# Pair writes of a routed MoE kernel moved to slots of their own, with GpSimd in text order

## Chip, core and metric

One core of a Trainium2 chip runs the whole kernel. The metric is the device time of one execution in microseconds (us), as the median over the runs shown. Engines: PE (TensorE; PEld is its weight load), DVE (VectorE), ACT (ScalarE), POOL (GpSimd) and SP (SyncE, which issues the ordinary DMAs).

## What is computed

A decayed linear attention over 4 x 768 tokens feeds a two-layer MLP, and its output x (3072 tokens x 384) goes through a mixture of eight experts, each token to its best one:

```python
kt, vt, rt, wt = (k[:, :, t], v[:, :, t], r[:, :, t], w[:, :, t])
cur = np.einsum('bhd,bhe->bhde', u[None] * kt, vt)
y[:, :, t] = np.einsum('bhd,bhde->bhe', rt, state + cur)
state = wt[:, :, :, None] * state + np.einsum('bhd,bhe->bhde', kt, vt)
...
h = x @ w_in
g = np.maximum(h, 0.0) + alpha * np.minimum(h, 0.0)
x = g @ w_out
...
expert_idx = np.argmax(x @ w_gate, axis=1)
gate_w = probs[np.arange(N), expert_idx]
out[mask] = gate_w[mask, None] * (np.maximum(x[mask] @ w1[e], 0.0) @ w2[e])
```

## The kernel before, in words

**Tiles and stages.** The tokens form 24 attention tiles of 128, numbered 0 to 23, and 8 blocks of three tiles, numbered 0 to 7. A prologue computes tiles 0 to 2. The main loop then has 128 MLP steps, 16 for each block; a step is one piece of 128 hidden units: nine matmuls of the first layer (`p1`, L584, into `ph`), the activation (ACT `gn` L587, DVE `gt` L589, ACT `gh` L595, DVE `gl` L597), and two steps later nine matmuls of the second layer (`p2`, L610, into `py`). Every product is made of high and low parts, so weights and activations each come as a pair (`wih`/`wil`, `woh`/`wol`, `gh`/`gl`). After the MLP the experts run in units of 256 or 128 tokens.

**Slots.** A step has two slots, and other work is hung on slot numbers with `at_slot`: the attention of the tiles of the next block, the conversion of the MLP weights during block 0, and the routing of the block just finished. For tile t the attention steps that matter here are: `r` on GpSimd (L292, written as dm<-dm,ex); the scores on PE (L348), ACT copies `at` (L356) that GpSimd masks (L360); `rk` on GpSimd (L312 and L313), which DVE reduces to `c` (L318), which GpSimd multiplies into `cv` (L328); the state `st`, added on DVE (L394) and multiplied by the decay `pm` on GpSimd (L395); `pm` itself on ACT (L339), in a single buffer, so that the next `pm` waits for `st`; the output `x` on DVE (L424), which PE transposes into `px` (L435).

**Routing of a block.** `gate_block` (L462) hangs four things on slots: the gate logits (on DVE as `sink` L489 for blocks 0 to 5, on PE for the last two), `route`, `rank` and `scatter`. `scatter` computes for each of the block's 384 tokens its row in the DRAM table `metad` (`slot`, L543) and the pair of token number and gate weight (`meta`, L547 to L549), and then GpSimd writes the pairs with three indirect DMAs (L551), one for each tile. I call these sends 0, 1 and 2. They write the same DRAM tensor, so each waits until the one before it has landed. `slot` and `meta` come from a pool with two buffers per name.

**Order.** Inside `manual_schedule(engines=...)` the engines named keep the order of the program text; a scheduler orders the rest ahead of the run. In the main loop `ORDER1` names PE alone until six steps before the end of the MLP; from there `ORDER2` names PE and DVE. On the chip each engine takes its instructions in the order so fixed.

**Weights in block 0.** The MLP weights arrive in 16 pieces j (even: first layer, odd: second layer). Each goes through ACT (`v`, L203), three DVE operations (L207, L208, L211), ACT (the high part, L224) and DVE or, for odd j, GpSimd (the low part, L229: `wil` or `wol`). Piece j = 8 is first needed by step 8, and so on.

Of the kernel before, what the change touches and what calls it, by code (L numbers as in the profile page):

```python
# [12 lines left out]
I32 = mybir.dt.int32  # L13
# [26 lines left out]
NBLK = NTILE // NB  # L40
# [3 lines left out]
EARLY = -(-((NBLK - 1) * BN - E * (UNIT - 1)) // UNIT)  # L44
LAG = 2
EPE, EDVE = mybir.EngineType.PE, mybir.EngineType.DVE


ORDER0 = None
ORDER1 = {EPE}  # L50
ORDER2 = {EPE, EDVE}
SWITCH = -6

# [1 line left out]

PE_GATES = 2
GV = 4
WARM0 = 16
WL_OFF = 6
LOW_V = range(0, 16, 2)  # L60
# [36 lines left out]
def attention_mlp_moe(ctx, tc, dmaj, tmaj, ub, alpha, w_in, w_out, w_gate, w_gate_b, wexp, out):  # L97
    nc = tc.nc
    vec, act, pool, pe, sp = nc.vector, nc.scalar, nc.gpsimd, nc.tensor, nc.sync
# [5 lines left out]
    mp = ctx.enter_context(tc.tile_pool(name="mp", bufs=2))  # L105
# [7 lines left out]
    ap = att_stack.enter_context(tc.tile_pool(name="ap", bufs=2))  # L113

    x2d = dp.tile([NT + 1, DM], F32, name="x2d")
    metad = dp.tile([NSLOT, 2], I32, name="metad")
# [29 lines left out]
    def warm(n):  # L146

        w = ps_h.tile([128, NP * 96], F32, tag="ph", name="warm")
        for _ in range(n):
            pe.matmul(w, lhsT=ones[:PR, :], rhs=bmask.rearrange("p a e -> p (a e)"), start=True, stop=True)  # L150
# [12 lines left out]
    def w_tiles(g):  # L163
        for lst, nm in ((wi_h, "wih"), (wi_l, "wil")):
            lst.append(wp.tile([128, KC, 1024], F32R, tag="W", name=f"{nm}{g}"))
        for lst, nm in ((wo_h, "woh"), (wo_l, "wol")):
            lst.append(wp.tile([128, 8, DM], F32R, tag="W", name=f"{nm}{g}"))
# [294 lines left out]
    def gate_block(blk, x2, g0):  # L462
        nt = NB
        t0 = blk * NB
        cx = {}

        def tr(j):
            pa = ps_a.tile([128, KC, 128], F32, tag="pa", name="px2")
            for c in range(KC):
                pe.transpose(pa[:, c, :], x2[:, j, 128 * c : 128 * c + 128], ident)  # L470
            xt = mp.tile([128, KC, 128], F32, tag="x2t", name="x2t")
            act.copy(xt, pa)
            cx[j] = xt

        def lg(j):
            pl = ps_a.tile([128, E], F32, tag="pa", name="plg")
            for c in range(KC):
                pe.matmul(pl, lhsT=cx[j][:, c, :], rhs=wg_s[:, c, :], start=c == 0, stop=c == KC - 1)
            if j == 0:
                cx["l"] = mp.tile([128, nt, E], F32, tag="lg", name="lg")  # L480
            vec.tensor_copy(cx["l"][:, j, :], pl)

        def lv(j, h):

            if j == h == 0:
                cx["l"] = mp.tile([128, nt, E], F32, tag="lg", name="lg")
            sink = mp.tile([128, DM], F32, tag="x2t", name="sink")
            for e in range(E // 2):
                vec.scalar_tensor_tensor(  # L489
                    out=sink,  # L490
                    in0=x2[:, j, :],
                    scalar=1.0,
                    in1=wgb_t[h][:, e, :],
                    op0=ALU.mult,
                    op1=ALU.mult,
                    accum_out=cx["l"][:, j, h * (E // 2) + e : h * (E // 2) + e + 1],
                )

        def small(name, dt=F32, w=E):
            return mp.tile([128, nt, w], dt, tag="g_" + name, name="g_" + name)  # L500

        def bc(t):
            return t.to_broadcast([128, nt, E])

        iob = iom.rearrange("p (o e) -> p o e", o=1).to_broadcast([128, nt, E])

        def route():
            l = cx["l"]
            m = small("m", w=1)
            vec.tensor_reduce(out=m, in_=l, axis=AX.X, op=ALU.max)  # L510
            sh, eq = small("sh"), small("eq")
            vec.tensor_tensor(out=eq, in0=l, in1=bc(m), op=ALU.is_equal)
            vec.tensor_tensor(out=eq, in0=eq, in1=iob, op=ALU.mult)
            mi = small("mi", w=1)
            vec.tensor_reduce(out=mi, in_=eq, axis=AX.X, op=ALU.min)
            oh = small("oh", BF16)
            vec.tensor_tensor(out=oh, in0=bc(mi), in1=iob, op=ALU.is_equal)
            ac = mp.tile([128, nt + 1, E], BF16, tag="g_ac", name="g_ac")
            pool.tensor_copy(ac[:, 0, :], acc_t[-1])
            for j in range(nt):  # L520
                pool.tensor_tensor(out=ac[:, j + 1, :], in0=ac[:, j, :], in1=oh[:, j, :], op=ALU.add)
            acc_t.append(ac[:, nt, :])
            vec.tensor_tensor(out=sh, in0=l, in1=bc(m), op=ALU.subtract)
            act.activation(sh, sh, AF.Exp)
            cx.update(sh=sh, mi=mi, oh=oh, ac=ac)

        def rank():
            oh, ac = cx["oh"], cx["ac"]
            pr = ps_a.tile([128, nt, E], F32, tag="pa", name="prk")
            fl = "p a e -> p (a e)"  # L530
            pe.matmul(pr.rearrange(fl), lhsT=tri, rhs=oh.rearrange(fl), start=True, stop=False)
            pe.matmul(pr.rearrange(fl), lhsT=ones, rhs=ac[:, 0:nt, :].rearrange(fl), start=False, stop=True)
            cx["pr"] = pr

        def scatter():
            sh, mi, oh, pr = cx["sh"], cx["mi"], cx["oh"], cx["pr"]
            rk = small("rk")
            vec.tensor_tensor(out=rk, in0=pr, in1=oh, op=ALU.mult)
            pos = small("pos", w=1)
            vec.tensor_reduce(out=pos, in_=rk, axis=AX.X, op=ALU.add)  # L540
            vec.tensor_scalar(mi, mi, float(NT), float(E * NT), op0=ALU.mult, op1=ALU.add)
            slot = small("slot", I32, 1)
            vec.tensor_tensor(out=slot, in0=pos, in1=mi, op=ALU.add)  # L543
            se = small("se", w=1)
            vec.tensor_reduce(out=se, in_=sh, axis=AX.X, op=ALU.add)
            vec.tensor_scalar(se, se, 1e-9, None, op0=ALU.add)
            meta = small("meta", I32, 2)  # L547
            pool.tensor_copy(meta[:, :, 0], tokid[:, t0 : t0 + nt])
            vec.reciprocal(out=meta.bitcast(F32)[:, :, 1:2], in_=se)  # L549
            for j in range(nt):  # L550
                pool.indirect_dma_start(  # L551
                    out=metad,
                    out_offset=bass.IndirectOffsetOnAxis(ap=slot[:, j, :], axis=0),
                    in_=meta[:, j, :],
                    in_offset=None,
                )

        g1 = g0 + 7
        if blk < NBLK - PE_GATES:
            for j in range(nt):  # L560
                for h in range(2):
                    at_slot(g0 + 1 + GV * (2 * j + h), lambda j=j, h=h: lv(j, h))
            g1 = g0 + 2 + 6 * GV
        else:
            for j in range(nt):
                at_slot(g0 + 2 + j, lambda j=j: tr(j))
                at_slot(g0 + 4 + j, lambda j=j: lg(j))
        at_slot(g1, route)
        at_slot(g1 + 2, rank)
        at_slot(g1 + 3, scatter)  # L570
        return g1 + 3

    g_t = {}
# [338 lines left out]
    def at_slot(s, fn):  # L912
        todo.setdefault(s, []).append(fn)
# [21 lines left out]
    at_slot(PT0, lambda: w_tiles(0))  # L935
    at_slot(PT0, lambda: warm(WARM0))
    for t, n in PRO_WARM:
# [48 lines left out]
    for i in range(len(steps) + LAG):  # L986
        if i == 0:
            order.close()
            tc.no_sync_barrier()
            order.enter_context(tc.manual_schedule(engines=ORDER1))  # L990
        if i == NM + SWITCH:
# [26 lines left out]
    with tc.For_i(0, nrem, 1) as iv:  # L1018
        tb = qp.tile([1, 1, 2], I32, tag="tb", name="tb", bufs=1)
        sp.dma_start(  # L1020
            out=tb, in_=tabd[:, ds(iv * 2, 2)].rearrange("p (o c) -> p o c", o=1)
# [71 lines left out]
```

## Time and profile before

| | |
|---|---|
| median of 3 runs | 877.07 us (875.84 to 878.21) |
| profiled execution, its own time | 875.71 us |
| span of that execution | 874.0 us |
| mean granted TensorE clock | 0.961 of full speed |
| busy: PE, DVE, ACT, POOL | 820.5, 645.4, 384.3, 293.4 us |

The span runs from the first to the last instruction; the time of the execution is 1.7 us longer. Times in the rows below are counted from the start of the span. The prologue lies at 0 to about 41 us, block 0 of the MLP at 41 to 140, the blocks after it up to about 607, the experts behind. In a timeline row the first number is the start, the second the duration, and the bracket at the end, where there is one, tells how long the engine sat idle before the row and what ended that wait.

### The profile page before, as it was taken

How to read it: one execution, taken by the hardware profiler on the slowest of the kernel's cores; microseconds unless marked ns; L12 is line 12 of the kernel's file. 1: busy time of each engine (PE TensorE's matmuls, PEld its weight loads, DVE VectorE, ACT ScalarE, POOL GpSimd, SP SyncE). 2: the span in 40 equal slices, each digit the busy share in tenths (PEclk: the TensorE clock that was granted, in tenths of full speed). 3: DMA queues.
4: the chain of work that ended last, by engine and by line, in shares of the span. 5: the costliest groups of instructions: out<-in, count | busy, mean ns of one | idle time of the engine just before them, and what ended most of it. 6: DMA issues, size and time to landing. Idle time of an engine off the chain costs nothing. (4 is left out here: it accounts for less than half of the span.)

```text
span 874.0 us, 14602 instructions
## 1 busy us (share of the span) xinstructions
PE 820.5 (94%) x5453; PEld 796.1 (91%) x5453; DVE 645.4 (74%) x1219; ACT 384.3 (44%) x751; POOL 293.4 (34%) x309
## 2 busy tenths in 40 slices
PE   6878789999799999999999999999999999999994
PEld 4768779999799999999999999999899999999993
DVE  6999898977686996896996983446767576776761
ACT  3545343344133433333333432337355556565641
POOL 5474444233332433343423330122224122232301
PEclk8779888999899999999999999999999999999997
DMA  9625534022212321311312300036456668585830
GB/s 281 203 83 171 193 120 148 29 60 86 59 59 60 87 60 60 86 60 60 86 60 59 87 1 1 28 137 242 147 202 240 224 216 293 204 294 204 275 119 21
DMA packets 30513, 111.59 MB, mean 128 GB/s; under 512 B 8229, under 2 KB 11592, under 8 KB 30440
## 3 DMA queue, kind: packets, MB, share of 16 engines
q1 hardware_dynamic: 26088, 100.38, 35.8%
q0 software_dynamic: 4352, 10.26, 3.2%
q8 instruction: 44, 0.72, 0.3%
q14 instruction: 29, 0.24, 0.1%
HBM read 100.95 MB, written 10.45 MB: 127 GB/s over the span
## 5 line engine op out<-in xcount | busy, mean ns | idle before, releaser
L584 PE MATMUL ph<-xth,wih 128*128 128x384 f32 x384 | 138.1, 360 | 8.4 <-DVE gt L589 5.2
L610 PE MATMUL py<-woh,gh 128*128 128x384 f32 x384 | 138.1, 360 | 1.0 <-ACT gh L595 1.0
L584 PE MATMUL ph<-xth,wil 128*128 128x384 f32 x384 | 132.9, 346 | 6.2 <-DVE wil L229 6.2
L595 ACT CAST gh<-gt 128x384 fp32r<-128x384 f32 x128 | 65.6, 513 | 158.5 <-DVE gt L589 158.5
L610 PE MATMUL py<-woh,gl 128*128 128x384 f32 x384 | 131.4, 342 | 1.4 <-DVE gl L597 1.4
L584 PE MATMUL ph<-xtl,wih 128*128 128x384 f32 x384 | 132.3, 345 | 0.0
L610 PE MATMUL py<-wol,gh 128*128 128x384 f32 x384 | 131.2, 342 | 0.0
L597 DVE TENSOR_TENSOR gl<-gt,gh 128x384 fp32r<-128x384 f32 x128 | 91.9, 718 | 33.3 <-ACT gh L595 31.8
L589 DVE SCALAR_TENSOR_TENSOR gt<-gn,oma_s,ph 128x384 f32<-128x384 f32 x128 | 76.4, 597 | 50.3 <-ACT gn L587 50.1
L587 ACT ACTIVATE gn<-ph 128x384 f32<-128x384 f32 x128 | 62.7, 490 | 113.2 <-PE ph L584 110.1
L815 DVE SCALAR_TENSOR_TENSOR gl<-ph,gh 128x256 fp32r<-128x256 f32 x96 | 40.4, 422 | 73.9 <-ACT gh L813 67.2
L489 DVE SCALAR_TENSOR_TENSOR sink<-x,wgb 128x384 f32<-128x384 f32 x144 | 88.1, 634 | 2.1 <-ACT x L621 1.4
L584 PEld LDWEIGHTS ph<-xth,wih 128*128 128x128 f32 x384 | 74.6, 194 | 10.3 <-DVE gt L589 5.8
L810 PE MATMUL ph<-xh,w1h 128*128 128x256 f32 x288 | 81.5, 283 | 1.2 <-DVE gl L815 1.1
L584 PEld LDWEIGHTS ph<-xth,wil 128*128 128x128 f32 x384 | 74.7, 194 | 7.4 <-DVE wil L229 7.4
L884 POOL DMA_INDIRECT out<-ys,meta x28 | 28.5, 1018 | 156.3 <-ACT ys L881 97.5
L810 PE MATMUL ph<-xl,w1h 128*128 128x256 f32 x288 | 80.8, 281 | 0.0
L810 PE MATMUL ph<-xh,w1l 128*128 128x256 f32 x288 | 80.4, 279 | 0.0
L610 PEld LDWEIGHTS py<-woh,gh 128*128 128x128 f32 x384 | 74.7, 195 | 3.0 <-ACT gh L595 1.3
L610 PEld LDWEIGHTS py<-woh,gl 128*128 128x128 f32 x384 | 74.1, 193 | 2.5 <-DVE gl L597 2.5
L584 PEld LDWEIGHTS ph<-xtl,wih 128*128 128x128 f32 x384 | 74.9, 195 | 0.8 <-DVE xtl L446 0.3
L610 PEld LDWEIGHTS py<-wol,gh 128*128 128x128 f32 x384 | 74.6, 194 | 0.0
(211 smaller groups left out, 1906.4 us busy)
## 6 DMA issues: line engine op xcount, KB each, us to landing
raw<-w SPq DMA_DIRECT2D x64, 768.0 KB
dm<-dmaj SPq DMA_DIRECT2D x21, 673.8 KB
tm<-tmaj SPq DMA_DIRECT2D x21, 576.0 KB
raw<-w_out SPq DMA_DIRECT2D x8, 768.0 KB
raw<-w_in SPq DMA_DIRECT2D x7, 768.0 KB
x2d<-x SPq DMA_DIRECT2D x8, 576.0 KB
both<-tmaj SPq DMA_DIRECT2D x3, 576.0 KB
wgb<-w_gate_b SPq DMA_DIRECT2D x2, 768.0 KB
```

The costliest lines, as they stand in the source:

```text
L489: vec.scalar_tensor_tensor(out=sink, in0=x2[:, j, :], scalar=1.0, in1=wgb_t[h][:, e, :], op0=ALU.mult, op1=ALU.mult, accum_out=cx["l"][:, ...
L584: pe.matmul(ph, lhsT=w, rhs=x[:, c, :], start=k == 0, stop=k == 3 * KC - 1)
L587: act.activation(gn, ph, AF.Relu, scale=-1.0)
L589: vec.scalar_tensor_tensor(out=gt, in0=gn, scalar=oma_s[:, f : f + 1], in1=ph, op0=ALU.mult, op1=ALU.add)
L595: act.copy(gh, gt)
L597: vec.tensor_tensor(out=gl, in0=gt, in1=gh.bitcast(F32), op=ALU.subtract)
L610: pe.matmul(y_t[blk][j], lhsT=g[:, sl], rhs=w, start=f == 0 and m == 0, stop=f == NF1 - 1 and m == 2,)
L810: pe.matmul(ph, lhsT=w, rhs=x, start=k == 0, stop=k == 3 * KC - 1)
L815: vec.scalar_tensor_tensor(out=gl, in0=ph, scalar=0.0, in1=gh.bitcast(F32), op0=ALU.max, op1=ALU.subtract)
L884: pool.indirect_dma_start(out=out, out_offset=bass.IndirectOffsetOnAxis(ap=d["meta"][:, j, 0:1], axis=0), in_=ys, in_offset=None, bounds_c ...
```

## The change

Four edits: `slot` and `meta` get one buffer per block (`NBLK` = 8) instead of two; the sends leave `scatter` and become a function of their own; for blocks 0 to 5 send j stands `SEND * j` = 0, 4 and 8 slots behind `scatter`, for the last two blocks all three stay at its slot; and GpSimd joins PE in `ORDER1`, so it keeps the text order up to the switch.

```diff
-ORDER1 = {EPE}
+ORDER1 = {EPE, EPOOL}
...
+SEND = 4
...
-            slot = small("slot", I32, 1)
+            slot = mp.tile([128, nt, 1], I32, tag="g_slot", name="g_slot", bufs=NBLK)
...
-            meta = small("meta", I32, 2)
+            meta = mp.tile([128, nt, 2], I32, tag="g_meta", name="g_meta", bufs=NBLK)
             pool.tensor_copy(meta[:, :, 0], tokid[:, t0 : t0 + nt])
             vec.reciprocal(out=meta.bitcast(F32)[:, :, 1:2], in_=se)
-            for j in range(nt):
-                pool.indirect_dma_start(
-                    out=metad,
-                    out_offset=bass.IndirectOffsetOnAxis(ap=slot[:, j, :], axis=0),
-                    in_=meta[:, j, :],
-                    in_offset=None,
-                )
+            cx.update(slot=slot, meta=meta)
+
+        def send(j):
+            pool.indirect_dma_start(
+                out=metad,
+                out_offset=bass.IndirectOffsetOnAxis(ap=cx["slot"][:, j, :], axis=0),
+                in_=cx["meta"][:, j, :],
+                in_offset=None,
+            )
...
         at_slot(g1 + 3, scatter)
+        for j in range(nt):
+            at_slot(g1 + 3 + (SEND * j if blk < NBLK - PE_GATES else 0), lambda j=j: send(j))
```

The order of PE's instructions stays as it was. Those of GpSimd, and with them those of DVE and ACT, which the scheduler places around it, move. Three places show it; line numbers of the changed kernel are larger by 3 to 5.

**GpSimd at the sends of block 0, before.** `cv` and `r` of tiles 9 and 10 stand ahead of the first row, and the last copy `g_meta` belongs to a later block.

```order
L312 TENSOR_TENSOR rk<-tm 128x384
L313 TENSOR_TENSOR rk<-rk,ub_s 128x384
L551 DMA metad<-g_meta,g_slot 24832x2 x2
L360 AFFINE_SELECT at_2024<-at_2024 128x512
L360 AFFINE_SELECT at_2027<-at_2027 128x512
L551 DMA metad<-g_meta,g_slot 24832x2
L548 COPY g_meta<-tokid 128x3
L395 TENSOR_TENSOR st<-st,pm 112x384
L328 TENSOR_TENSOR cv<-tm,c 128x384
```

**The same place now.**

```order
L551 COPY g_meta<-tokid 128x3
L556 DMA metad<-g_meta,g_slot 24832x2
L331 TENSOR_TENSOR cv<-tm,c 128x384
L363 AFFINE_SELECT at_2022<-at_2022 128x512
L363 AFFINE_SELECT at_2025<-at_2025 128x512
L295 TENSOR_TENSOR dm<-dm,ex 112x512
L556 DMA metad<-g_meta,g_slot 24832x2
L398 TENSOR_TENSOR st<-st,pm 112x384
L315 TENSOR_TENSOR rk<-tm 128x384
L316 TENSOR_TENSOR rk<-rk,ub_s 128x384
L556 DMA metad<-g_meta,g_slot 24832x2
L331 TENSOR_TENSOR cv<-tm,c 128x384
```

The masks of tile 9 and its `st` now stand between the sends and not behind the second and third; the two products `rk` of tile 10 stand behind send 1 and `st`, where they stood ahead of send 0. No copy `g_meta` for a later block stands behind send 2.

**DVE between `st` and `x` of tile 9, before and now.** The sinks are the gate logits of block 0.

```order
L394 TENSOR_TENSOR st<-pv,st 112x384
L489 SCALAR_TENSOR_TENSOR sink,lg<-x_2048,wgb 128x384 x3
L589 SCALAR_TENSOR_TENSOR gt<-gn,oma_s,ph 128x384
L489 SCALAR_TENSOR_TENSOR sink,lg<-x_2048,wgb 128x384 x2
L597 TENSOR_TENSOR gl<-gt,gh 128x384
L489 SCALAR_TENSOR_TENSOR sink,lg<-x_2048,wgb 128x384
L424 TENSOR_TENSOR x<-py,cv 128x384
```

```order
L397 TENSOR_TENSOR st<-pv,st 112x384
L492 SCALAR_TENSOR_TENSOR sink,lg<-x_2046,wgb 128x384 x3
L596 SCALAR_TENSOR_TENSOR gt<-gn,oma_s,ph 128x384
L321 TENSOR_REDUCE c<-rk 128x8
L492 SCALAR_TENSOR_TENSOR sink,lg<-x_2046,wgb 128x384
L604 TENSOR_TENSOR gl<-gt,gh 128x384
L492 SCALAR_TENSOR_TENSOR sink,lg<-x_2046,wgb 128x384
L427 TENSOR_TENSOR x<-py,cv 128x384
```

The reduction `c` of tile 10, which reads `rk` of that tile, now stands ahead of `x` of tile 9. It stood some fifteen rows earlier. The same exchange is found at blocks 2 and 4.

**GpSimd in block 0 of the MLP, before and now** (attention of tiles 3 and 4; `wol` are the low parts of pieces 3, 5 and 7).

```order
L519 COPY g_ac<-acc_117 128x8
L548 COPY g_meta<-tokid 128x3 x2
L328 TENSOR_TENSOR cv<-tm,c 128x384
L312 TENSOR_TENSOR rk<-tm 128x384
L292 TENSOR_TENSOR dm<-dm,ex 112x512
L313 TENSOR_TENSOR rk<-rk,ub_s 128x384
L360 AFFINE_SELECT at_539<-at_539 128x512
L229 TENSOR_TENSOR wol_121<-v_496,woh_120 128x768
L360 AFFINE_SELECT at_542<-at_542 128x512
L395 TENSOR_TENSOR st<-st,pm 112x384
L229 TENSOR_TENSOR wol_121<-v_586,woh_120 128x768
L229 TENSOR_TENSOR wol_121<-v_693,woh_120 128x768
```

```order
L331 TENSOR_TENSOR cv<-tm,c 128x384
L363 AFFINE_SELECT at_539<-at_539 128x512
L363 AFFINE_SELECT at_542<-at_542 128x512
L232 TENSOR_TENSOR wol_121<-v_496,woh_120 128x768
L295 TENSOR_TENSOR dm<-dm,ex 112x512
L398 TENSOR_TENSOR st<-st,pm 112x384
L315 TENSOR_TENSOR rk<-tm 128x384
L316 TENSOR_TENSOR rk<-rk,ub_s 128x384
L232 TENSOR_TENSOR wol_121<-v_586,woh_120 128x768
L232 TENSOR_TENSOR wol_121<-v_693,woh_120 128x768
```

The three small copies at the head go to their blocks, and `rk` and `dm` of tile 4 move behind the masks and `wol` of piece 3. On DVE the reduction `c` of tile 5, which stood right ahead of the low part `wil` of piece 8, goes some thirty rows back, and a reciprocal of tile 5 takes its place.

## Rows read from the trace of the kernel before

**Rows 1.** Busy time by stretch: length, PE, PEld, DVE, ACT, POOL, PEclk, DMA share, GB/s.
```profile
300.00:400.00 100.00, 100.00 (x680) 97.52 (x679) 83.25 (x194) 37.07 (x88) 39.45 (x47) 1.00 0.21 63
```
**Rows 2.** PE's waits from 90 to 300 us: total, times, longest.
```profile
PE px L435 <- DVE x L424: 6.6, 2, 6.1
PE ph L584 <- DVE wil L229: 6.2, 3, 5.0
```
**Rows 3.** Timeline of POOL around the sends of block 0.
```profile
205.78 1.01 POOL L312 TENSOR_TENSOR rk<-tm 128x384 f32<-128x384 f32 x1
206.88 1.51 POOL L313 TENSOR_TENSOR rk<-rk,ub_s 128x384 f32<-128x384 f32 x1
209.55 1.20 POOL L551 DMA_INDIRECT metad<-g_meta,g_slot  x1 [1.17 <-DVE rec L305]
216.85 0.96 POOL L551 DMA_INDIRECT metad<-g_meta,g_slot  x1 [6.09 <-DMA metad<-g_meta,g_slot]
217.82 1.82 POOL L360 TENSOR_SCALAR_AFFINE_SELECT at<-at 128x512 f32<-128x512 f32 x2
222.28 0.98 POOL L551 DMA_INDIRECT metad<-g_meta,g_slot  x1 [2.64 <-DMA metad<-g_meta,g_slot]
228.40 0.18 POOL L548 COPY g_meta<-tokid 128x3 int32<-128x3 int32 x1 [5.14 <-DMA metad<-g_meta,g_slot]
228.54 0.99 POOL L395 TENSOR_TENSOR st<-st,pm 112x384 f32<-112x384 f32 x1
```
**Rows 4.** Timeline of ACT in the same stretch.
```profile
217.49 0.51 ACT L595 CAST gh<-gt 128x384 fp32r<-128x384 f32 x1 [0.86 <-DVE gt L589]
229.57 0.37 ACT L339 ACTIVATE pm<-bmask,ex 112x96 f32<-112x96 bf16 x1 [11.57 <-POOL st L395]
```
**Rows 5.** Timeline of DVE in the same stretch.
```profile
219.97 0.54 DVE L394 TENSOR_TENSOR st<-pv,st 112x384 f32<-112x384 f32 x1
...
230.35 0.62 DVE L589 SCALAR_TENSOR_TENSOR gt<-gn,oma_s,ph 128x384 f32<-128x384 f32 x1 [8.40 <-ACT gn L587]
...
232.79 0.55 DVE L424 TENSOR_TENSOR x<-py,cv 128x384 f32<-128x384 f32 x1
```
**Rows 6.** Timeline of PE in the same stretch.
```profile
225.61 0.33 PE L610 MATMUL py<-woh,gh 128*128 128x384 f32 x1
...
227.00 0.34 PE L610 MATMUL py<-woh,gl 128*128 128x384 f32 x1
233.40 0.90 PE L435 MATMUL px<-ident,x 128*128 128x128 f32 x3 [6.06 <-DVE x L424]
...
234.41 0.52 PE L584 MATMUL ph<-xtl,wih 128*128 128x384 f32 x1
...
238.57 0.49 PE L610 MATMUL py<-woh,gl 128*128 128x384 f32 x1
```
**Rows 7.** POOL's waits over the whole span: total, times, longest.
```profile
POOL metad L551 <- DMA metad<-g_meta,g_slot: 41.8, 15, 6.1
```
**Rows 8.** Timeline of DVE at the same point of block 2.
```profile
366.82 0.55 DVE L424 TENSOR_TENSOR x<-py,cv 128x384 f32<-128x384 f32 x1
```
**Rows 9.** Timeline of PE at the same point of block 2.
```profile
367.71 0.49 PE L435 MATMUL px<-ident,x 128*128 128x128 f32 x3
```
**Rows 10.** Timeline of DVE in block 0 of the MLP.
```profile
52.45 4.88 DVE L211 SCALAR_TENSOR_TENSOR v<-raw,v 128x768 uint32<-128x768 uint32 x1
...
90.74 0.55 DVE L318 TENSOR_REDUCE c<-rk 128x8 f32<-128x384 f32 x1 [2.50 <-POOL rk L313]
91.21 1.45 DVE L229 TENSOR_TENSOR wil<-v,wih 128x768 fp32r<-128x768 f32 x1
...
96.25 0.94 DVE L301 RECIPROCAL rec<-ex 112x128 f32<-112x128 f32 x1
```
**Rows 11.** Timeline of PE in block 0 of the MLP.
```profile
92.72 0.69 PE L584 MATMUL ph<-xth,wil 128*128 128x384 f32 x1 [4.98 <-DVE wil L229]
```
**Rows 12.** Instructions of line 211: shortest, median and longest in ns, first and last start.
```profile
L211 DVE SCALAR_TENSOR_TENSOR v<-raw,v x15: 944/948/4876, 29.1 to 131.3; 128x768 uint32<-128x768 uint32 x15
```

More of the change, by code (lines that the diff above doesn't have):

```diff
@@ L46 @@
 EPE, EDVE = mybir.EngineType.PE, mybir.EngineType.DVE
+EACT, EPOOL = mybir.EngineType.Activation, mybir.EngineType.Pool
 ORDER0 = None
-ORDER1 = {EPE}
+ORDER1 = {EPE, EPOOL}
 ORDER2 = {EPE, EDVE}
```

## The prediction

> **What bounds the kernel now.** I read the busy time by stretch first. From 300 to 400 us PE is busy for all of 100 us at the granted clock 1.00, which is the 2.4 GHz level [rows 1]; in such a stretch no wait of another engine costs anything, and a faster GpSimd gains nothing. So the question is where PE is not at that level. The list of PE's waits from 90 to 300 us has two entries that matter: 6.1 us at once for `px`, the transposes of an attention tile's output, released by DVE's `x`, and 6.2 us in three waits (the longest 5.0) for `wil`, the low part of an MLP weight piece [rows 2]. GpSimd's own largest wait on the sends is 41.8 us in 15 pieces [rows 7]; that is a wait of an engine that is mostly idle, and the reader should not count it as a gain. What matters is which of these pieces PE feels.
>
> One does. At block 0 send 0 runs from 209.55 to 210.75 us. Send 1 waits for its landing until 216.85, the two masks of tile 9 stand behind send 1, send 2 waits again until 222.28, and a small copy `g_meta` for a later block, whose buffer send 2 still reads, holds the queue until 228.40. Only then does the state product `st` run, at 228.54 [rows 3]. Its input was ready when DVE's `st` ended, 219.97 + 0.54 = 220.51 us [rows 5]: 8.0 us late. ACT stands idle 11.57 us before `pm`, which waits for `st`, and the `gn` of an MLP step is behind that `pm` [rows 4]. DVE's `gt` waits 8.40 us for that `gn`, and `x` of tile 9 stands behind `gt` in DVE's order and comes at 232.79 [rows 5]. PE, in its fixed order, has finished at 227.34 and begins `px` at 233.40 after 6.06 us of nothing [rows 6]. Behind that wait the matmuls start 0.32 us apart (13 steps from 234.41 to 238.57, the 1.2 GHz level), where ahead of it they started 0.174 apart (8 steps from 225.61 to 227.00, the 2.4 GHz level) [rows 6]. With the last one some 15 matmuls run at the lower level, 15 x 0.146 = 2.2 us. The stall costs 6.06 + 2.2 = 8.3 us.
>
> **The change, part by part.**
>
> *Sends apart, numbers with a buffer per block, at block 0.* Nothing is added or removed: 24 sends before and after. The new order puts `cv`, the masks and `r` between send 0 and send 1, `st` and the two `rk` of tile 10 between 1 and 2. If send 0 lands as it did, send 1 goes out at 216.85 again and is through at 217.81 [rows 3], 2.7 us ahead of the end of DVE's `st` at 220.51 [rows 5]. So `st` runs at 220.5 to 221.5 and `pm` begins at 221.5, not 229.57 [rows 4]. The masks come earlier as well. Then `rk` takes 1.01 + 1.51 us [rows 3], to 224.0, and DVE's `c` of tile 10, 0.55 us [rows 10], which now stands ahead of `x`, ends at 224.6. Three more DVE operations follow, which I take at the 0.47 that lies between the starts of `c` and `wil` [rows 10], then `x`, 0.55: it ends near 226.6, and PE wants it at 227.34 [rows 6]. The 8.3 us go, with 0.7 us to spare. Send 2 follows `rk` at 224, after its own release at 222.28 [rows 3], and holds nobody. The `g_meta` copy for a later block no longer stands there; its wait of 5.14 us [rows 3] goes with the new buffers.
>
> *Sends of the other blocks.* There is no PE wait to remove in the full stretch [rows 1]: gain 0. The cover is the slack of `x`. At block 2 `x` ends at 366.82 + 0.55 = 367.37 and `px` begins at 367.71 [rows 8, 9]: 0.34 us. I put the cost at 0, since `st` there gets earlier too, and come back to it under the rivals. For the last two blocks the three sends stay together, and the order around them is as before: 0.
>
> *GpSimd in text order in block 0 of the MLP.* Here DVE is the engine that PE waits for [rows 2], and the order of three engines moves, so this is the uncertain term. Two places can be priced.
>
> First, 90.74 us: DVE waited 2.50 us for GpSimd's `rk` before `c` of tile 5, and `wil` came right behind, at 91.21; PE waited 4.98 us for it, until 92.72 [rows 10, 11]. The changed order takes `c` away from there: 2.50 us and 91.21 - 90.74 = 0.47 go. A reciprocal takes its place, which lasted 0.94 where it stood before [rows 10]. Net 2.50 + 0.47 - 0.94 = 2.0 us earlier. Below, the gain could be 0, if DVE gives the time back at its next wait for PE; above, 4.98, if the whole wait goes. I take the 2.0 that is counted.
>
> Second, 52.45 us: one L211 operation took 4.88 us there [rows 10], where the median of its line is 0.948 [rows 12], while GpSimd ran the copies, `cv`, `rk` and `dm` without a gap. The operation is 3.9 us longer for it. In the new order the masks wait for ACT there and leave GpSimd a gap, so up to 3.9 us could go. But `rk` and `dm` don't vanish: they come behind `wol` and `st`, where DVE is just as busy, and may hold it there for as long. Bounds: gain 3.9, loss 3.9. I take 0, as the same work meets the same full engine.
>
> The Trainium skill, SBUF — State Buffer, section "Who interferes with whom", says that a VectorE operation with two SBUF inputs and a GpSimd operation that reads SBUF exclude each other for one whole instruction. By that rule alone a hold would last at most the longer `rk`, 1.51 us [rows 3], the bounds of this term would be 1.5 either way, and the rival on bursts would come to 870.5. The row disagrees with its 3.9, and I go by the row.
>
> *Sum.* 8.3 + 2.0 = 10.3 us. The profiled execution took 875.71 us (span 874.0 and 1.7 around it): 875.71 - 10.3 = 865.4. That execution lies 1.36 us below the median of 877.07, so against the median I forecast **866.8 us**. Nothing after the MLP is late for it: the order of all engines in the expert phase stays, and it shifts forward whole.
>
> **The rivals.**
>
> *GpSimd's new bursts hold DVE in block 0 of the MLP.* `st`, `rk`, `rk`, `wol` now follow each other, and later `wol`, mask, mask, `dm`. If one more burst does to DVE what the one at 52.45 did (3.9 us), PE waits that much longer and runs some 15 matmuls at the lower level behind it (2.2): 866.8 + 6.1 = **872.9 us**. For it: DVE has no slack where PE waits for `wil` [rows 2]. Against: the burst at 52.45 breaks up.
>
> *The first block gives all it has.* The wait of 4.98 us vanishes with its stretch at the lower level (2.2), 7.2 us and not 2.0: 866.8 - 5.2 = **861.6 us**. For it: GpSimd's early idle copies leave, and `rk` of tile 5 is off DVE's path. Against: `x` of tile 4 now stands ahead of a `wil` as well, and DVE then waits for PE.
>
> *The stall stays.* If send 0 lands later than 220.51 us, 9.8 us after it was issued and not 6.1 [rows 3], send 1 again stands ahead of `st` and the change doesn't do what it is built for: 866.8 + 8.3 = **875.1 us**. It needs a landing 3.7 us slower.
>
> *`c` ahead of `x` makes a wait of its own.* In blocks 0, 2 and 4 `c` of the next tile now stands on DVE ahead of `x`, and needs `rk`, which stands on GpSimd behind send 1 and `st`. `x` has 0.7 us to spare at block 0 by my count and 0.34 at block 2 in the trace [rows 8, 9]; from there on PE waits. Let `x` be 3 us late, half of today's wait: each such place costs 3 + 2.2 = 5.2 us, block 0 gains 8.3 - 5.2 = 3.1 only, blocks 2 and 4 lose 10.4, and with the 2.0 of the first block the sum is 5.3 us slower than before: **882.4 us**. For it: the slack is thin. Against: in blocks 2 and 4 `st` waits for no landing now, so `rk` and `c` should end in time.
>
> The Trainium skill, Perfetto Trace Analysis, section "Tensor Engine Instruction (MATMUL, LD_WEIGHTS)", notes that DVE, ACT and GpSimd are strict FIFO. That is the rule that speaks against a fixed GpSimd order; the wait of 8.0 us in which a ready `st` stood behind a copy agrees with it.
>
> **How the numbers follow.** Forecast 0.60; the bursts 0.17; the first block in full 0.10; the stall stays 0.05; `c` ahead of `x` 0.08. The forecast's own range is 863 to 871, the 3.9 us either way. The range of 860 to 874 takes in the bursts and the full first block, and leaves out the two last cases and the tails. A measurement of this kernel can tell 0.3%, 2.6 us, from no change: faster means below 874.4. Faster 0.85 (the first three cases, less a little of the bursts), the same 0.08 (most of "the stall stays" and the mild form of `c` ahead of `x`), slower 0.07.
>
> **What would show it.** Right: no idle time of PE before `px` between 200 and 240 us and the granted clock 1.00 there; `st` of tile 9 on GpSimd within 1 us of DVE's `st`; `pm` no longer the longest wait of ACT; the wait for `wil` of piece 8 near 3 us. Wrong: DVE operations of 3 us and more between 60 and 75 or 95 and 130 us, a PE wait for `px` at blocks 2 or 4, or a first block that ends later than 140 us. If GpSimd's waits on landings fall by tens of microseconds and the time by no more than 10, that is as expected.

## The result and the profile after

The changed kernel takes **865.87 us** (median, 864.35 to 867.8), the kernel before 876.99 in the same session: ratio 0.9863, 95% interval 0.9829 to 0.9897, 11.1 us faster. The forecast was 866.8 us. The profiled execution took 865.37 us (span 863.6), 10.3 us under that of before.

Three places are compared: block 0's sends, the first MLP block, and the rest. Busy time by stretch in the changed kernel (columns as in [rows 1]: busy us and count of PE, PEld, DVE, ACT, POOL, then the granted clock):

```profile
40.00:90.00 50.00, 36.07 (x215) 33.81 (x215) 48.02 (x59) 26.62 (x51) 31.80 (x28) 0.86 0.38 134
90.00:140.00 50.00, 42.01 (x254) 39.30 (x253) 48.27 (x64) 22.46 (x41) 26.93 (x15) 0.93 0.47 162
...
200.00:240.00 40.00, 40.00 (x273) 38.80 (x271) 35.16 (x85) 13.87 (x31) 17.50 (x16) 1.00 0.22 52
```

The same stretches of the kernel before, which [rows 1] does not show:

```profile
40.00:90.00 50.00, 38.40 (x211) 35.48 (x209) 45.97 (x55) 26.72 (x51) 29.14 (x32) 0.82 0.38 131
90.00:140.00 50.00, 42.42 (x219) 40.41 (x220) 47.10 (x61) 21.05 (x38) 21.58 (x15) 0.80 0.49 162
...
200.00:240.00 40.00, 33.94 (x209) 32.87 (x208) 27.80 (x64) 11.32 (x26) 14.41 (x15) 0.91 0.26 72
```

From 200 to 240 us PE no longer idles and stays at clock 1.00, where it lost 6.06 us and ran at 0.91. In the first block (40 to 140 us) PE is idle for 21.9 us of 100 after and 19.2 before, and still does more, 469 matmul records for 430: in this pair of traces the gain came as clock, 0.81 to 0.90, which is less time at the 1.2 GHz level, and not as waits. A second trace of the kernel before (experiment 8) warns against reading more into one pair. There PE is idle for 23.8 us at a clock of 0.84:

```profile
40.00:90.00 50.00, 38.18 (x213) 35.34 (x213) 44.77 (x56) 24.64 (x49) 24.35 (x28) 0.81 0.35 119
90.00:140.00 50.00, 38.06 (x211) 35.95 (x210) 46.98 (x59) 22.10 (x38) 24.68 (x17) 0.88 0.52 167
```

GpSimd at block 0 in the changed kernel (timeline: start, duration, line, output and inputs, idle time before it and its releaser), against [rows 3]:

```profile
205.59 1.19 POOL L556 DMA_INDIRECT metad<-g_meta,g_slot  x1 [8.12 <-DVE dm L310]
206.82 1.05 POOL L331 TENSOR_TENSOR cv<-tm,c 128x384 f32<-128x384 f32 x1
208.08 1.22 POOL L363 TENSOR_SCALAR_AFFINE_SELECT at<-at 128x512 f32<-128x512 f32 x2 [0.22 <-ACT at L359]
209.28 1.18 POOL L295 TENSOR_TENSOR dm<-dm,ex 112x512 f32<-112x512 f32 x1
212.67 1.29 POOL L556 DMA_INDIRECT metad<-g_meta,g_slot  x1 [2.21 <-DMA metad<-g_meta,g_slot]
216.09 1.23 POOL L398 TENSOR_TENSOR st<-st,pm 112x384 f32<-112x384 f32 x1 [2.12 <-DVE st L397]
```

Its DVE, ACT and PE at the same place, against [rows 4 to 6]:

```profile
215.44 0.55 DVE L397 TENSOR_TENSOR st<-pv,st 112x384 f32<-112x384 f32 x1
...
219.92 0.55 DVE L321 TENSOR_REDUCE c<-rk 128x8 f32<-128x384 f32 x1 [0.38 <-POOL rk L316]
...
221.81 0.55 DVE L427 TENSOR_TENSOR x<-py,cv 128x384 f32<-128x384 f32 x1
```

```profile
217.35 0.38 ACT L342 ACTIVATE pm<-bmask,ex 112x96 f32<-112x96 bf16 x1 [2.70 <-POOL st L398]
```

```profile
223.85 0.49 PE L438 MATMUL px<-ident,x 128*128 128x128 f32 x3
```

`st` runs 0.1 us after its input (215.99 to 216.09), where it was 8.0 late. ACT waits 2.70 us before `pm`, not 11.57. `x` ends at 222.36, 1.5 us ahead of PE's `px`, which shows no wait at all. The wait of 0.38 us of `c` for `rk` is the mechanism of one rival, `c` ahead of `x`: it is there, and `x` has room for it.

### Where the time went, by a mark that every trace has

PE's order is fixed, so its transposes `px` mark the same points of the work in every trace (us; tiles counted from 0). Tile 8's is the last ahead of block 0's sends. There are 24 tiles; the group of such rows that comes 26th, the transposes for the gates of the last block, is called tile 25 here and in the expectations, and its last row is taken. The last column is the profiled execution's time.

| kernel | tile 2 | tile 8 | tile 11 | tile 25 | 8 to 25 | to the span's end | time |
|---|---|---|---|---|---|---|---|
| before | 39.76 | 204.13 | 278.62 | 611.82 | 407.7 | 262.2 | 875.7 |
| before, second trace | 42.66 | 208.00 | 281.32 | 614.68 | 406.7 | 263.5 | 880.0 |
| changed | 39.84 | 200.75 | 266.63 | 600.64 | 399.9 | 263.0 | 865.4 |
| buffers alone (experiment 1) | 39.82 | 205.65 | 272.15 | 605.57 | 399.9 | 261.5 | 868.8 |

Tile 2's mark lies ahead of the first block, tile 11's behind block 0's sends. Against the execution that the prediction started from, the change is 3.4 us ahead at tile 8, gains 8.6 at block 0's sends (tile 8 to 11), and loses 0.8 from there to tile 25 and 0.8 behind it. Against the mean of both traces of before it is 5.3 ahead at tile 8 and gains 7.3 from there to tile 25.

The stretch from tile 2 to tile 8 holds the first block and none of block 0's sends. The four traces with GpSimd in the old order in that block (both of before, experiments 1 and 3) take 164.4 to 165.8 us for the stretch, the five with the text order in all of the block (the changed kernel, experiments 2, 4, 6 and 7) 159.6 to 161.8. The two groups don't overlap, and their means lie 4.5 us apart.

### The profile page after: what moved, and what is told of

The parts are those of the page before. It is cut to its first block, busy times and chain, and to the rows that moved or that the text cites. A ratio compares the mean times of both kernels' runs of the same rounds, so it can differ in the third digit from the quotient of the medians.

```text
span 863.6 us, 14591 instructions
## 1 busy us (share of the span) xinstructions
PE 812.2 (94%) x5453; PEld 787.7 (91%) x5453; DVE 640.4 (74%) x1219; ACT 385.0 (45%) x751; POOL 298.4 (35%) x309
## 5 line engine op out<-in xcount | busy, mean ns | idle before, releaser
L591 PE MATMUL ph<-xth,wih 128*128 128x384 f32 x384 | 136.3, 355 | 11.1 <-DVE gt L596 9.0
L591 PE MATMUL ph<-xth,wil 128*128 128x384 f32 x384 | 131.0, 341 | 4.8 <-DVE wil L232 4.8
L617 PE MATMUL py<-wol,gh 128*128 128x384 f32 x384 | 129.4, 337 | 0.0
L604 DVE TENSOR_TENSOR gl<-gt,gh 128x384 fp32r<-128x384 f32 x128 | 86.4, 675 | 32.9 <-ACT gh L602 31.3
L492 DVE SCALAR_TENSOR_TENSOR sink<-x,wgb 128x384 f32<-128x384 f32 x144 | 98.8, 711 | 1.5 <-ACT x L628 1.2
L363 POOL TENSOR_SCALAR_AFFINE_SELECT at<-at 128x512 f32<-128x512 f32 x46 | 37.2, 830 | 112.1 <-ACT at L359 112.1
```

The lines of the kernel that those rows point to most:

```text
L363: pool.affine_select(out=cx[jj], in_=cx[jj], pattern=[[0, NP], [1, 128]], compare_op=ALU.is_gt, fill=0.0, base=0, channel_multiplier=-1,)
L492: vec.scalar_tensor_tensor(out=sink, in0=x2[:, j, :], scalar=1.0, in1=wgb_t[h][:, e, :], op0=ALU.mult, op1=ALU.mult, accum_out=cx["l"][:, ...
L591: pe.matmul(ph, lhsT=w, rhs=x[:, c, :], start=k == 0, stop=k == 3 * KC - 1)
L604: vec.tensor_tensor(out=gl, in0=gt, in1=gh.bitcast(F32), op=ALU.subtract)
L617: pe.matmul(y_t[blk][j], lhsT=g[:, sl], rhs=w, start=f == 0 and m == 0, stop=f == NF1 - 1 and m == 2,)
```

## The experiments

Times are medians; the ratio is to the kernel before, run beside it (877.47, 877.83 and 878.12 us in the three sessions).

**1. Buffers alone.** The kernel before with

```
-            slot = small("slot", I32, 1)
+            slot = mp.tile([128, nt, 1], I32, tag="g_slot", name="g_slot", bufs=NBLK)
...
-            meta = small("meta", I32, 2)
+            meta = mp.tile([128, nt, 2], I32, tag="g_meta", name="g_meta", bufs=NBLK)
```

> The kernel before, with the one edit that slot and meta have a buffer per block. The order of GpSimd differs from before only in that the six g_meta copies of later blocks leave the places behind the sends and stand with the first two. Theory (st is held by what stands ahead of it, and most of that is the copy, which waits for send 2): st of tile 9 goes right behind send 2, at about 222.3 + 1.2 = 223.5 us and not 228.5, ACT's pm and DVE's x come 5.1 us earlier, PE waits about 6.06 - 5.1 = 1 us for px, and most of the 2.2 us at the lower clock go too: about 868.5 to 870 us, 7 to 8 under before. The first block is as before (c waits 2.5 us for rk, PE 5 us for wil). Rival 1 (the spacing of the sends is what removes the stall): PE still waits over 4 us for px, 874 to 877. Rival 2 (all the gain was the stall, the first block gave nothing): 866.

Measured: 871.62 us, ratio 0.9935 (0.9912 to 0.9957). GpSimd at block 0 in this run:

```profile
217.49 1.31 POOL L551 DMA_INDIRECT metad<-g_meta,g_slot  x1 [5.23 <-DMA metad<-g_meta,g_slot]
218.81 1.60 POOL L360 TENSOR_SCALAR_AFFINE_SELECT at<-at 128x512 f32<-128x512 f32 x2
223.48 0.98 POOL L551 DMA_INDIRECT metad<-g_meta,g_slot  x1 [3.06 <-DMA metad<-g_meta,g_slot]
224.49 1.01 POOL L395 TENSOR_TENSOR st<-st,pm 112x384 f32<-112x384 f32 x1
```

and its PE:

```profile
229.36 0.55 PE L435 MATMUL px<-ident,x 128*128 128x128 f32 x3 [0.48 <-DVE x L424]
```

The sends still stand together and `st` still waits for two landings, but the copy for a later block is gone, and with it all but 0.48 us of PE's 6.06. `st` ran 1 us later than expected, in a run that stood 1.5 us later than the first trace of before already at tile 8, and the wait was half of what was expected. Between tiles 8 and 25 this run takes 399.9 us, as the changed kernel. The theory holds for the place. The time is 1.6 us over its range: the profiled execution took 868.8, among the fastest of twelve, so what the slower ones add is not in a trace.

The sends' spacing does nothing by itself: with GpSimd in the scheduler's order, the kernel with the sends apart has the same instructions in the same order on every engine as the one without. Two traces show it: behind the first block, from 150 us on, this run (sends together) and experiment 4 (sends apart) have the same order on all four engines. Slots order only what is issued in the order of the text.

**2. Text order alone.** The kernel before with `ORDER1 = {EPE, EPOOL}`, the sends together.

> The kernel before, with GpSimd in the order of the text and nothing else: the three sends of a block follow each other directly, two buffers. Theory (the sends must be apart): the first block gains what the change gains there, 3 to 5 us by 200 us; at block 0 sends 1 and 2 wait some 6 and 5 us for landings, cv, both masks, r and st of tile 9 stand behind them, so st runs near 225 us, 8 to 9 us after it is ready, and the masks some 12 us later than in the changed kernel: PE waits 5 us or more between 215 and 235 us, and some at the other blocks where the masks stand behind the sends: 870 to 880 us. Rival (the text order alone does it, the spacing is not needed): 865 to 867 us and no wait of PE over 2 us between 200 and 300.

Measured: 893.41 us, ratio 1.0176 (1.0143 to 1.0210). Slower than before, and by far more than expected. GpSimd at block 0:

```profile
202.96 1.19 POOL L552 DMA_INDIRECT metad<-g_meta,g_slot  x1 [8.13 <-DVE dm L308]
209.22 0.96 POOL L552 DMA_INDIRECT metad<-g_meta,g_slot  x1 [5.07 <-DMA metad<-g_meta,g_slot]
215.51 0.96 POOL L552 DMA_INDIRECT metad<-g_meta,g_slot  x1 [5.33 <-DMA metad<-g_meta,g_slot]
216.50 0.84 POOL L329 TENSOR_TENSOR cv<-tm,c 128x384 f32<-128x384 f32 x1
217.28 1.22 POOL L361 TENSOR_SCALAR_AFFINE_SELECT at<-at 128x512 f32<-128x512 f32 x2
```

PE's waits (engine, tile and line, releaser: us in total, times, longest) and its stretch from 140 to 560 us:

```profile
PE py L415 <- POOL at L361: 9.5, 6, 3.2
PE px L436 <- DVE x L425: 3.1, 2, 2.0
```

```profile
140.00:560.00 420.00, 403.42 (x2604) 391.93 (x2603) 306.94 (x720) 142.12 (x326) 133.38 (x159) 0.96 0.19 58
```

The masks stand behind three sends and PE waits for them, six times. At tile 8 this run is the earliest of all (198.12), and then it loses 33 us to tile 25 against the changed kernel: 16.6 us of idle PE and 403 x 0.04 = 16 us of clock. Only 8.3 of the 33 are lost at block 0 (tile 8 to 11), where `st` ran at 219.61 and not near 225. What the expectation missed is the price of the blocks behind, and of the clock, which it doesn't name. The run has the two buffers of before as well; experiment 6 shows that in text order they cost nothing.

**3. Text order from step 16 on.** The changed kernel, first block in the old order:

```
-ORDER1 = {EPE, EPOOL}
+ORDER1 = {EPE}
+ORDER1B = {EPE, EPOOL}
+TEXT_FROM = 16
...
+        if i == TEXT_FROM:
+            order.close()
+            order.enter_context(tc.manual_schedule(engines=ORDER1B))
```

> The changed kernel, but GpSimd goes over to the order of the text only at step 16, so the first block (to about 140 us) is in the order of the kernel before. Theory (the gain has two parts, the stall at block 0 and the first block): the stall is gone as in the changed kernel, the first block's part is missing: 865.9 + 3.4 (what the changed kernel has gained by 200 us) = 869.3, by the forecast's term 865.9 + 2.0 = 867.9. Rival (the first block's gain is given back in the stretches behind it): 866 us, as the changed kernel.

Measured: 871.54 us, ratio 0.9939 (0.9912 to 0.9967). No PE wait at block 0, tile 8 at 205.28, as before. The missing first block costs 871.54 - 865.87 = 5.7 us by the medians; the theory holds with a larger size than either figure given.

**4. Text order in the first 16 steps only**, then the scheduler's, with the buffers (the same edit with the two sets of engines exchanged).

> The changed kernel, but GpSimd is in the order of the text only in the first 16 steps, then in the scheduler's order, with a buffer per block. Theory (two parts, and the buffers alone remove nearly all of the stall): the first block as in the changed kernel, st of tile 9 behind send 2, about 1 us of PE wait for px: 866 to 868 us. Rival (only the text order with the sends apart removes the stall): 865.9 + 6 to 8 = 872 to 874 us.

Measured: 865.63 us, ratio 0.9871 (0.9840 to 0.9903), as the changed kernel. PE waits 2.1 us for `px` at block 0, twice what was expected and four times the 0.48 of experiment 1, whose order this is behind the first block:

```profile
224.73 0.55 PE L440 MATMUL px<-ident,x 128*128 128x128 f32 x3 [2.06 <-DVE x L429]
```

GpSimd's waits for the landings of sends 0 and 1 were 6.46 and 4.09 us here, 5.23 and 3.06 there, and from tile 8 to 25 this run takes 403.1 us, 3.2 more than the changed kernel. So by the times, text order with sends apart and scheduler's order with buffers are worth the same behind the first block; by these two traces the second still hands part of a slow landing on to PE.

**5. Where in the first block: text order from step 5, and from step 8.** The edit of 3 with 5 and 8 in place of 16.

> The changed kernel, GpSimd in the order of the text from step 5 on (about 75 us); the order before that, with the unbroken row of GpSimd operations at 52 us, is as before, while c of tile 5 has left its place ahead of wil of piece 8, as in the changed kernel. Read by PE's first transpose of tiles 3 and 4 (before and the two runs with the old order in the first block: 74.0 to 75.1 and 107.3 to 108.1 us; the three runs with the text order: 70.8 to 72.6 and 99.1 to 101.6). Theory (most of the first block's gain is made between these two, where c no longer holds wil): tile 3 near 74.4, tile 4 near 74.4 + 28.7 = 103 us, time 868 us. Rival (the gain comes from the operation of 4.88 us at 52 us, and c is worth the counted 2.0 or less): tile 4 at 105.8 or later, time 870 us.

> The changed kernel, GpSimd in the order of the text from step 8 on: c of tile 5 still stands ahead of wil of piece 8, as before. Theory (c ahead of wil is the place): PE waits some 5 us for wil of piece 8, the first transpose of tile 4 near 107 us, time 870 to 871.5 us, as with the old order in the whole first block. Rival (the gain comes from the later places, masks, rk and wol behind 90 us): tile 4 near 104, time 867 to 868 us.

Measured: 867.19 us (ratio 0.9874, 0.9830 to 0.9919) and 869.16 us (0.9910, 0.9874 to 0.9947). From step 8, `c` still stands ahead of `wil`; its DVE and its PE:

```profile
93.17 0.55 DVE L323 TENSOR_REDUCE c<-rk 128x8 f32<-128x384 f32 x1 [2.49 <-POOL rk L318]
93.64 1.45 DVE L234 TENSOR_TENSOR wil<-v,wih 128x768 fp32r<-128x768 f32 x1
```

```profile
95.14 0.69 PE L593 MATMUL ph<-xth,wil 128*128 128x384 f32 x1 [5.18 <-DVE wil L234]
```

This repeats [rows 10, 11]. With the times of 3 and of the changed kernel in a row (871.5, 869.2, 867.2, 865.9) steps 8 to 15 give 2.4 us, steps 5 to 7, with `c`, 2.0, and the first five 1.3. Each step is smaller than its interval, so this is a split by medians and not a proof. The marks don't bear it out: tile 4 came at 106.55 and 109.74, but in both runs tile 2, ahead of all that differs, was already 2.0 and 4.4 us later than in the first trace of before. Counted from tile 2 to tile 8 the two runs take 160.7 and 161.0 us, as the five with text order throughout. By this count steps 8 to 15 alone give nearly all of the gain, though PE's wait of 5.18 us for `wil` is still there. By the medians `c` and the later places give some 2 us each. These are two traces, one of each kernel, so which places of the block pay stays open.

**6. Changed kernel with the two buffers of before.**

> The changed kernel with the two buffers of before for slot and meta: text order and sends apart. Every engine has the same instructions in the same order as in the changed kernel, since the text puts each g_meta copy in its own block. Theory (in the order of the text the buffers are worth nothing): 865.9 us, within 1.5, no wait of GpSimd for a g_meta buffer. Rival (the copy waits for the send of two blocks earlier also there): 868 to 871 us with waits before g_meta.

Measured: 866.17 us, ratio 0.9866 (0.9819 to 0.9913); no wait of GpSimd for a `g_meta` buffer. In text order the buffers are worth nothing, since the copy stands in its own block, long behind the send it had waited for.

**7. Sends 2 half steps apart** (`SEND = 2`).

> The changed kernel with 2 half steps between a block's sends, not 4: send 1 stands behind the masks, r behind it, and send 2 right behind r. Theory (what counts is that no send whose predecessor has not landed stands ahead of st): send 1 is through at 213.8 as before, send 2 waits for it until about 219, st of tile 9 is ready at 216.0 and runs near 220, 4 us late; PE waits up to 3 us a block at several of the six blocks with sends apart: 868 to 882 us, I take 873. Rival (2 apart is as good as 4): 866 us and no PE wait over 1.5 us between 200 and 300.

Measured: 871.48 us, ratio 0.9935 (0.9911 to 0.9960). GpSimd at block 0:

```profile
212.24 1.21 POOL L295 TENSOR_TENSOR dm<-dm,ex 112x512 f32<-112x512 f32 x1
217.42 1.20 POOL L556 DMA_INDIRECT metad<-g_meta,g_slot  x1 [3.97 <-DMA metad<-g_meta,g_slot]
218.64 1.01 POOL L398 TENSOR_TENSOR st<-st,pm 112x384 f32<-112x384 f32 x1
```

and the input of that `st` on DVE:

```profile
216.24 0.55 DVE L397 TENSOR_TENSOR st<-pv,st 112x384 f32<-112x384 f32 x1
```

Send 2 again stands ahead of `st`, which is 1.9 us late and not 4, and PE waits 5.5 us for `gt` and `px` in eight short pieces from 140 to 560 us, none over 1.2. From tile 8 to 25 this run takes 406.7 us, 6.8 more than the changed kernel. Each piece is small; together they take back half of the gain. The theory holds, with shorter waits than the 3 us that it allowed a block.

**8. The kernel before, a second trace.**

> The kernel before, unchanged, for a second trace of it. Read by PE's first transpose of tiles 8 and 25 (first trace of before: 204.13 and 611.82, 407.7 between; all runs in which st does not stand behind the copy and the sends: 399.3 to 400.4 between). Theory (the stall is in every execution and worth 8 us; the profiled execution of before was early by 1 to 1.5 us at tile 8): tile 8 near 205, 407 to 408.5 between, time 876 to 878. Rival (the stall of 6.06 us is not in every execution, which is why the times of the runs without it lie only 5.9 under before): less than 405 between.

Measured: 878.68 us, ratio 0.9997 (0.9974 to 1.0020). PE waits 5.9 us for `px` at block 0 and 5.0 for `wil`, as in [rows 2]: both are in both traces of this kernel. From tile 8 to 25 it took 406.7 us, a little under the theory's 407 and over the rival's 405. Tile 8 came at 208.00, 3 us later than expected and 3.9 later than in the first trace. Of that, 2.9 us are there at tile 2 already, ahead of the first block; from tile 2 to 8 the two traces differ by 1.0 us. So a gain in the first block is to be counted from tile 2 and not from the start of the span.

**9. Three tries for more**, on the changed kernel: low parts of pieces 12 and 14 on GpSimd (`LOW_V = (0, 2, 4, 6, 8, 10)`), DVE in text order, ACT in text order (`EDVE` or `EACT` added to `ORDER1`).

> The changed kernel, the low parts of w_in pieces 12 and 14 (two 128x768 subtractions of the first block) on GpSimd and not on DVE. Theory (the first block is bound by DVE, busy 48.3 of 50 us from 90 to 140, GpSimd 26.9): DVE is 2 x 0.9 us shorter, PE waits less for x and gt, 863 to 865.5 us. Rival (the operation takes 2 to 4 us on GpSimd beside a full DVE, as wol does, and PE waits for these low parts instead): 867 to 871 us.

> The changed kernel, DVE in the order of the text as well, up to the experts (where it already is). Theory (the text order pays where the scheduler's order puts a waiting operation ahead of one that PE needs, as c ahead of wil; but the text says nothing of when things come free, and DVE has 8 times the number of operations of GpSimd there): the first block waits more, the sinks keep away from gt and x: 866 to 880 us, I take 870. Rival (the text is the better order also for DVE): 858 to 864 us.

> The changed kernel, ACT in the order of the text as well. ACT is busy under half of the time from 140 us on (22 to 23 of 50 us in the first block). Theory (ACT is not what PE waits for, and its order changes little): 865 to 868 us. Rival (in a fixed order pm and kt stand ahead of gn and gh, which PE needs at once, and every wait of ACT for GpSimd is handed on to PE): 870 us or more, with PE waits for gh and gt after 140 us.

Measured: 872.43 us (0.9931, 0.9904 to 0.9959), 893.60 (1.0151, 1.0120 to 1.0183), 895.01 (1.0186, 1.0159 to 1.0212). One of the two moved low parts took 4.16 us on GpSimd in the first:

```profile
111.09 4.16 POOL L232 TENSOR_TENSOR wil<-v,wih 128x768 fp32r<-128x768 f32 x1 [4.50 <-ACT wih L227]
```

With DVE in text order PE waits 17.0 us for `px` in the first block:

```profile
PE px L438 <- DVE x L427: 17.0, 2, 8.7
```

With ACT in text order it waits for ACT's copy of `x` behind it (140 to 560 us):

```profile
PE ph L591 <- ACT xth L444: 7.0, 6, 3.2
```

So the first theory falls, and the rival's low part at 4.16 us is there; the time is 1.4 us over the rival's range too. DVE in text order is as bad as the theory said in direction, and 27.7 us slower than the changed kernel where 4 were expected. (The expectation's 8 times the operations of GpSimd are 4 times: 1219 to 309 in the trace of the changed kernel.) For ACT the theory falls and the rival holds, mostly by a copy that it had not named. None beats the changed kernel, which with 4 and 6 is the fastest found.

## Why the prediction was right

- **The stall at block 0, 8.3 us.** Right. PE's wait and the lower clock behind it went. From tile 8 to 11 the changed kernel takes 65.9 us, the two traces of before 74.5 and 73.3: 8.6 and 7.4 us. Every sign named for it came: no idle before `px`, clock 1.00, `st` 0.1 us late, ACT's wait 2.70. By times alone the stall is 5.9 us (experiment 1; by its interval 3.8 to 7.7). The rest of that difference stays open.
- **Which edit removes it.** The prediction took the three edits as one. They are two alternatives: the buffers alone remove all but 0.5 us of PE's wait in one trace and all but 2.1 in another (experiments 1 and 4), and text order with sends apart removes it without the buffers (experiment 6). The price of 5.14 us on the copy's wait [rows 3] stood in the prediction, as something that "goes with the new buffers", and was nearly the whole effect at this place.
- **Other blocks, 0.** Right at a spacing of 4: no PE wait for `px` at blocks 2 or 4, and 0.8 us lost from tile 11 to 25. Experiments 2 and 7 show what this cover is worth: without it the sends of all six blocks cost 33 us and 7, of which 25 and 4 fall behind tile 11.
- **The first block, 2.0 us.** Mis-sized. Measured 3.4 in the one pair, 5.7 by times (experiment 3), 4.5 by the nine traces from tile 2 to 8. What failed is the sum for this block: one counted place, the burst term at 0 "as the same work meets the same full engine", and no term for the clock. From 40 to 140 us the four traces with the old order there show PE idle for 19.2 to 24.3 us at a mean clock of 0.81 to 0.85, the five with text order in all of it 17.6 to 21.9 us at 0.86 to 0.90. In the means that is 2.2 us of waits and 79 x 0.043 = 3.4 us of clock, which no term had. (Their sum is over the 4.5: the four reach tile 2 1.3 us later in the mean, which this window counts.) Whether the counted place gave its 2.0 is open: by the medians of experiment 5 it did, by the marks it gave next to nothing.
- **Why the sum fits.** In the pair of traces 8.3 + 2.0 stands against 8.6 at the sends, 3.4 in the first block, and 1.6 lost behind tile 11, which the sum had at 0. By times the two parts are 5.9 and 5.7. In either count errors of opposite sign lie in a total that is off by 0.9 us, so that it is this near is in part luck.
- **The rivals.** The bursts didn't hold DVE: none of its operations from 60 to 130 us lasts 3 us, and the one of 4.88 us at 52.45 [rows 10] has gone. GpSimd pays for them, as two rows of the changed kernel show:

```profile
68.06 3.24 POOL L316 TENSOR_TENSOR rk<-rk,ub_s 128x384 f32<-128x384 f32 x1
...
94.33 3.96 POOL L232 TENSOR_TENSOR wol<-v,woh 128x768 fp32r<-128x768 f32 x1 [4.09 <-ACT woh L227]
```

  The stall that stays did not come: send 1 ran at 212.67, 7.1 us behind send 0. `c` ahead of `x` came at 0.38 us. The first block in full was nearer in size than its 0.10: by times the block gave 5.7 of that rival's 7.2. Its mechanism, the whole wait for `wil` gone, did not come: 2.34 us are left.
- **The wait for `wil` of piece 8.** Forecast near 3 us, where it had been 4.98 [rows 11]; in the changed kernel it is this:

```profile
89.26 0.44 PE L591 MATMUL ph<-xth,wil 128*128 128x384 f32 x1 [2.34 <-DVE wil L232]
```

- The Trainium skill, Perfetto Trace Analysis, section "Tensor Engine Instruction (MATMUL, LD_WEIGHTS)", has DVE, ACT and GpSimd as strict FIFO. Experiment 7's rows agree: `st`, whose input was ready at 216.79, runs at 218.64, right behind a send that sat 3.97 us waiting for a landing.

## What to carry to other kernels

When a ready operation stands behind a waiting one, look for the smallest edit that moves the waiting one: here, at the sends, more buffers for a tiny copy did nearly what a new order of a whole engine did. Fixing an engine's order by the text is a choice with a duty: each thing in it that waits for a landing must then be put apart by hand, or the same change costs 16 us (experiment 2) instead of gaining 11. And where PE waits often and briefly, size an edit by the granted clock of the stretch as well as by the waits, from more than one trace, and between two marks of the same work.

## What the hardware showed that was not expected

- Short waits of PE can cost double, or only themselves. In experiment 2 16.6 us of idle time came with 16 us of lower granted clock, from waits of at most 3.2 us. In experiment 7 6.9 us in waits of at most 1.3 us left the clock at 1.00, and with ACT in text order (experiment 9) 16.1 us in waits of at most 3.2 us left it at 0.99. So the total of the waits doesn't give their price. The stretch of experiment 7, beside the one shown under experiment 2:

```profile
140.00:560.00 420.00, 413.11 (x2763) 402.04 (x2762) 322.30 (x753) 151.01 (x349) 141.30 (x170) 1.00 0.20 60
```

- The first block gained more by clock than by waits, 3.4 us against 2.2 in the means of nine traces; single pairs scatter too widely to show it.
- An operation of DVE or GpSimd can stretch beside the other engine by more than one operation of that engine. `wol` took 1.81 us at 43.76, where it was DVE's operation that was held (3.32 us at 42.80, line 210, against 0.55 at 93.31), and 3.96 at 94.33. Beside the second, DVE ran these without a gap:

```profile
94.30 0.95 DVE L211 SCALAR_TENSOR_TENSOR v<-raw,v 128x768 uint32<-128x768 uint32 x1
95.17 0.55 DVE L604 TENSOR_TENSOR gl<-gt,gh 128x384 fp32r<-128x384 f32 x1
95.64 0.95 DVE L214 SCALAR_TENSOR_TENSOR v<-raw,v 128x768 uint32<-128x768 uint32 x1
```

  They end at 96.59, and `wol` ends 1.70 us later, near its 1.81. That reads as one GpSimd operation held by three of DVE in a row, which is argued from the times and not shown by an experiment. The Trainium skill, SBUF — State Buffer, section "Who interferes with whom", has the ports that the two engines share as an exclusive lock, held for a whole instruction. The added 2.15 us is more than any one of DVE's operations there (1.56 at most), so a single such hold doesn't give the row; several in turn would. The prediction's 1.51 us from that section counted a single one.
